# First expert slots five steps sooner, their tables on VectorE, and one test at the kernel's end

## The chip, the cores and the metric

The kernel runs on one core of a Trainium2 chip. The metric is the device time of one execution in microseconds (us). The kernel before takes 1280.56 us (median of three runs, 1279.65 to 1280.75).

## The reference, cut to what matters

Attention of 8 batches x 8 heads over 576 tokens with head size 64, in which each query keeps its 32 best keys, and then a mixture of 8 experts with one expert per token:

```python
scores = scale * (q @ k.T)                       # 576 x 576 for each batch and head
mask = scores >= (32nd largest of the row)
attn = softmax(where(mask, scores, -1e9)); o = attn @ v
x = o, heads side by side                        # 4608 tokens x 512
logits = x @ w_gate; e = argmax(logits); p = softmax(logits)[e]
out[tok] = p * sigmoid(x[tok] @ w_output_gate[:, e]) * (relu(x[tok] @ w1[e]) @ w2[e])   # 512 -> 1024 -> 512
```

## The kernel before, in words

**The loop.** The 4608 tokens are 36 query tiles of 128, and a step takes one pair of heads of one tile, so there are 144 steps (`NSTEP`), and the loop over `i` (L873) runs four more for what trails. Everything is written into the engines' instruction streams in the order of this loop; each engine runs its own stream in order and waits for the others by semaphores. In a step VectorE finds each row's 32nd largest score: `rank` (six MAX8 at L308 and four MATCH_REPLACE at L311, here for step i; the first L308 of six marks a step's start), `window` (two MAX8 at L350, step i-1), `gmax` (sixteen MAX8 at L301, step i+1), `choose` (two small operations at L361, step i-1; in calm steps also L365, a limit for ScalarE) and `weigh` (L377, which drops the scores below the limit and sums the rest). ScalarE copies the scores from PSUM (L282), makes marks (L335), takes the exponentials (L345, in calm steps L393 for the second head) and copies the turned probabilities (L412). GpSimd (POOL in the profile) adds the marks to the scores (L338, two additions a step). TensorE makes the scores (L274), turns the probabilities (`flip`, L404) and in every second step multiplies them with v (`attend`, L436).

**Calm steps.** In the steps below `LONE` (= 4 x 7 + 20 = 48) the second head's mask is not made by VectorE's `weigh` but by ScalarE (L384) and GpSimd (L387, the addition of `veil`), which saves VectorE one L377 a step. TensorE has no expert work in these steps.

**Routing.** When a tile's four steps are done, its gate logits are made (L466, L475 on TensorE, `tile_rows` on VectorE). `SORTS` names after which tiles the tokens so far are sorted by expert: the groups end at tiles 7, 10, 12 and so on, with 3, 2, 3 ... slots each, and after the last tile come `USUAL` = 11 slots (40 in all). A slot is 128 tokens of one expert. For a group, `group_route` is some 22 small VectorE operations (L520 to L566), and `slot_table` (L581) some 28 dependent operations on a few numbers that say which expert a slot has and where its tokens lie. The table runs on GpSimd for the nine groups inside the loop, and on VectorE for the last. `queue_slots` then appends the slots to `order`.

**What sets the order.** Small operations stand in queues: `fill(n)` writes n of them from `urgent`, then `small`, into VectorE's stream at the place where it is called: in a calm step four after `choose` and four at the step's end (L951, L960). `later("ids", ...)` (L863) puts work on GpSimd under a budget per step (`run_slow`). `side` holds TensorE work of the router.

**A slot's work.** Once in `order`, a slot passes through `ahead(...)`: list of tokens (`id`), weights (`w1`, `w2`, 2 MB each by SyncE's queue), the rows (`x`, a gather of GpSimd), the turned rows (`turn`, L703 on TensorE). `ahead("x", fetch_x, 2, "id", 2)` says that x is fetched two steps after id at the soonest. Then `heavy_start` puts four pieces in a queue and the loop takes one per step (`heavy_piece`): two up products (L714, 32 matmul records each) and two down products (L729, eight records). The output is scattered by GpSimd (L740).

**The tail.** After the loop come the heavy pieces left, then the other slots in `slots_in_turn`, with weights and rows split in two parts of lower precision (ScalarE L1008, VectorE L1009, products L1036). At the very end `unsettled` counts rows whose 32nd largest is not certain. Then every engine loads `need` (L1155) and branches if more than the usual 11 last slots are called for (L1157), and loads `flag` (L1171) and branches if a row was unsettled (L1173), in which case all is done again exactly. With the data of this benchmark neither branch's body runs.

Of the kernel before, what the change touches and what calls it, by code (L numbers as in the profile page):

```python
# [13 lines left out]
I32 = mybir.dt.int32  # L14
# [12 lines left out]
SORTS = ((7, 3, 112), (10, 2, 96), (12, 3, 120), (15, 3, 80), (17, 4, 96), (20, 1, 128), (23, 4, 112), (27, 4, 128),  # L27
# [12 lines left out]
def tile_topk_attention_moe(  # L40
# [65 lines left out]
    before = consts.tile([P, P], F32, name="before")  # L106
# [23 lines left out]
    def setup():  # L130
# [5 lines left out]
        def gates():  # L136
            for a in range(2):
# [8 lines left out]
        ops = [lambda: nc.gpsimd.memset(wg, 0.0), gates,  # L146
               lambda: nc.gpsimd.memset(ones, 1.0), lambda: nc.gpsimd.memset(ones_b, 1.0),
               iota(before, [[1, P]], 0, -1),
               lambda: nc.gpsimd.tensor_scalar(before_b, before, 0.0, None, op0=ALU.is_gt),
# [12 lines left out]
    flag = consts.tile([1, 1], I32, name="flag")  # L162

    def unsettled(cp, pp):
# [17 lines left out]
        nc.vector.tensor_copy(flag, total)  # L182

    def run(exact, stack):
# [11 lines left out]
        pools = {"p": ps_m}  # L196
# [118 lines left out]

        def lone(i, a):
            return a == 1 and not exact and i < LONE
# [263 lines left out]
        def slot_table(g, last):  # L581
# [3 lines left out]
            eng = nc.vector if last else nc.gpsimd  # L585
# [30 lines left out]
            if last:  # L616
                def count():
                    NEED.append(st.tile([1, 1], I32, name="need"))
                    eng.tensor_copy(NEED[0], T["d"][:, 7 + E:8 + E])
                add(count)  # L620
# [7 lines left out]
            for k in (4, 2, 1):  # L628
                for nm in ("past", "way"):
                    add(lambda nm=nm, k=k: eng.tensor_tensor(T[nm][:, :n, 0:k], T[nm][:, :n, 0:k], T[nm][:, :n, k:2 * k],  # L630
                                                             op=ALU.add))
            add(lambda: eng.tensor_scalar(tl("slot", [1, 2, MAXS])[:, 0, :n], T["past"][:, :n, 0], float(E - 1), None,
                                          op0=ALU.min))
            add(lambda: eng.tensor_tensor(T["way"][:, :n, 0], T["way"][:, :n, 0], slot_off[:, :n], op=ALU.add))
            add(lambda: eng.tensor_tensor(T["slot"][:, 1, :n], T["way"][:, :n, 0],
                                          first_row[:, 0:1].to_broadcast([1, n]), op=ALU.add))
            def slots():
                SLOT[g] = st.tile([1, 2, MAXS], I32, name="slots", bufs=3)
                eng.tensor_copy(SLOT[g][:, :, :n], T["slot"][:, :, :n])
# [19 lines left out]
        gbuf = [mp.tile([P, DM], F32, name=f"xg{g}", bufs=1) for g in range(NGB)]  # L659
        for x in gbuf:  # L660
            nc.gpsimd.memset(x, 0.0)
# [4 lines left out]
        def fetch_w1(s, g, k, rows):  # L666
            ev = nc.values_load(SLOT[g][0:1, 0, k:k + 1], engines=[SP], min_val=0, max_val=E - 1,
                                skip_runtime_bounds_check_because="clamped to the last expert")
            a = mp.tile([P, NC, FF], F32, name="w1t", bufs=2)
# [3 lines left out]
        def fetch_w2(s, g, k, rows):  # L673
            ev = nc.values_load(SLOT[g][0:1, 0, k:k + 1], engines=[SP], min_val=0, max_val=E - 1,
                                skip_runtime_bounds_check_because="clamped to the last expert")
            b = mp.tile([P, NF, DM], F32, name="w2t", bufs=2)
# [3 lines left out]
        def fetch_id(s, g, k, rows):  # L680
# [3 lines left out]
            it = mp.tile([P, 4], I32, name="idt", bufs=NLIST)  # L684
# [14 lines left out]
        def turn(s, pool, name):  # L699
# [4 lines left out]
            def ev():  # L704
                XS[s] = mp.tile([P, NC, P], F32, name="xs", bufs=2)
                nc.scalar.activation(XS[s], px, AF.Copy)
# [11 lines left out]
        def up(s, f0):  # L718
            if f0 == 0:
                HT[s] = mp.tile([P, NF, P], F32, name="ht")  # L720
# [11 lines left out]
        def put(s):  # L732
            it = G[s][0]
            flush("out")
            y = mp.tile([P, DM], F32, name="y", bufs=2)
# [16 lines left out]

        LONE = 4 * ENDS[0] + 20 if ENDS else 0
# [119 lines left out]
        for i in range(NSTEP + 4):  # L873
# [6 lines left out]
            calm = i < LONE and not exact  # L880
# [26 lines left out]
            elif 2 <= i < LONE:  # L907
# [25 lines left out]
            if ev:  # L933
                late.append(ev)
# [283 lines left out]
```

## Time and profile before

| | |
|---|---|
| median of three runs | 1280.56 us (1279.65 to 1280.75) |
| the profiled execution | 1277.66 us, span 1275.8 us |
| busy share of the span | TensorE (PE) 92%, VectorE (DVE) 94%, ScalarE (ACT) 82%, GpSimd (POOL) 59% |
| TensorE's granted clock | 0.986 of full speed in the mean |
| HBM | 178 GB/s over the span |

Busy times of all engines but TensorE are those of instructions, not of useful work: an instruction that is held up while it runs counts as busy. TensorE's matmuls are pipelined and their ends modelled, so its waits tell more than its busy time. The span is 1.9 us shorter than the execution's own time.

### The profile page before, as it was taken

What the parts mean: (1) busy time and instruction counts of PE and PEld (TensorE: products, weight loads), DVE (VectorE), ACT (ScalarE), POOL (GpSimd) and SP (SyncE); (2) the same over time, 40 slices, a digit from 0 to 9 for tenths busy, and PEclk for the clock granted to TensorE, in tenths of its full rate; (3) what the DMA queues carried; (4) which work ended last, traced back from release to release, by engine and by line L of the source; (5) the groups of instructions that cost most, each with busy time, mean ns of one, the idle gap of its engine ahead of it and who ended that gap; (6) DMA issues with size and microseconds to landing.
All of it is one profiled execution on the core that took longest, in us unless ns stands there. A gap on an engine that the chain in (4) does not pass through costs nothing. (4 is left out here: it accounts for less than half of the span.)

```text
span 1275.8 us, 31308 instructions
## 1 busy us (share of the span) xinstructions
PE 1179.8 (92%) x9792; PEld 898.1 (70%) x9792; DVE 1197.4 (94%) x6154; ACT 1043.8 (82%) x1984; POOL 755.4 (59%) x1221
## 2 busy tenths in 40 slices
PE   6888778677799999999999999999999999999995
PEld 5665656555577777777777777777777777788884
DVE  7999999999999999999999999999999974898884
ACT  6999999898888878788888888888888863888883
POOL 6666666698775766756767667567657743311210
PEclk8999999999799999999999999999999999999998
DMA  5400210202818562765565565765554467999980
GB/s 138 77 18 25 65 55 18 55 19 64 289 54 279 199 228 106 242 228 158 173 204 158 210 208 156 263 221 185 192 176 150 157 233 251 380 396 378 382 312 32
DMA packets 109383, 227.47 MB, mean 178 GB/s; under 512 B 14858, under 2 KB 33546, under 8 KB 108176
## 3 DMA queue, kind: packets, MB, share of 16 engines
q1 hardware_dynamic: 99536, 205.67, 48.1%
q0 software_dynamic: 7552, 18.96, 4.4%
q8 instruction: 81, 1.33, 0.5%
q10 hardware_dynamic: 2112, 0.68, 0.3%
q14 instruction: 102, 0.84, 0.2%
HBM read 206.68 MB, written 20.69 MB: 178 GB/s over the span
## 5 line engine op out<-in xcount | busy, mean ns | idle before, releaser
L338 POOL TENSOR_TENSOR w<-s,marks 128x576 f32<-128x576 f32 x288 | 362.9, 1281 | 181.7 <-ACT marks L335 171.2
L301 DVE MAX8 cand<-s 128x8 f32<-128x72 f32 x2304 | 322.1, 218 | 9.7 <-ACT s L282 9.7
L404 PE MATMUL pst<-ident,ep 128*128 128x128 f32 x1296 | 207.0, 284 | 55.1 <-ACT ep L393 47.1
L335 ACT ACTIVATE marks<-s,v 128x576 int8<-128x576 f32 x288 | 220.9, 770 | 35.8 <-DVE v L308 31.9
L404 PEld LDWEIGHTS pst<-ident,ep 128*128 128x128 f32 x1296 | 145.9, 142 | 142.5 <-ACT ep L393 57.8
L412 ACT ACTIVATE pT<-pst 128x512 f32<-128x512 f32 (+1 forms) x432 | 197.8, 481 | 7.0 <-PE pst L404 4.6
L350 DVE MAX8 v<-w 128x8 f32<-128x576 f32 x288 | 202.2, 744 | 0.0
L282 ACT ACTIVATE s<-ps 128x1152 f32<-128x1152 f32 (+1 forms) x145 | 162.3, 1120 | 45.5 <-PE ps L274 44.2
L714 PE MATMUL pm<-xs,w1t 128*128 128x128 f32 x1664 | 194.7, 275 | 0.9 <-issue 0.8
L714 PEld LDWEIGHTS pm<-xs,w1t 128*128 128x128 f32 x1664 | 189.9, 192 | 1.4 <-issue 1.1
L377 DVE SCALAR_TENSOR_TENSOR ep<-s,kth,ep 128x576 f32<-128x576 f32 x240 | 188.0, 812 | 0.3 <-issue 0.3
L274 PE MATMUL ps<-kst,qst 64*128 64x288 f32 (+1 forms) x1280 | 181.4, 432 | 5.4 <-ACT s L282 5.4
L436 PE MATMUL po<-pT,v 128*64 128x128 f32 (+3 forms) x3200 | 185.1, 266 | 0.0
L436 PEld LDWEIGHTS po<-pT,v 128*64 128x64 f32 (+1 forms) x3200 | 157.8, 136 | 33.0 <-issue 31.3
L729 PE MATMUL pm<-w2t,ht 128*128 128x512 f32 x400 | 180.4, 594 | 0.0
L345 ACT ACTIVATE ep<-s,v 128x576 f32<-128x576 f32 x240 | 175.4, 778 | 0.0
L740 POOL DMA_INDIRECT out_dram<-y,idt x40 | 45.4, 1136 | 184.6 <-ACT y L736 167.3
L308 DVE MAX8 v<-cand 128x8 f32<-128x64 f32 x864 | 148.3, 213 | 0.0
L274 PEld LDWEIGHTS ps<-kst,qst 64*128 64x128 f32 (+1 forms) x1280 | 98.2, 178 | 44.6 <-issue 16.2
L729 PEld LDWEIGHTS pm<-w2t,ht 128*128 128x128 f32 x400 | 72.2, 190 | 72.4 <-issue 72.4
L311 DVE MATCH_REPLACE8 cand<-v,cand 128x64 f32<-128x64 f32 x576 | 116.2, 209 | 0.0
L387 POOL TENSOR_TENSOR w<-s,marks 128x576 f32<-128x576 f32 x48 | 61.5, 1280 | 52.7 <-ACT marks L384 52.4
(182 smaller groups left out, 1838.0 us busy)
## 6 DMA issues: line engine op xcount, KB each, us to landing
w1t<-in_w_dram SPq DMA_DIRECT2D x40, 2048.0 KB
w2t<-in_w_dram SPq DMA_DIRECT2D x40, 2048.0 KB
v<-in_va_dram SPq DMA_DIRECT2D x8, 1152.0 KB
x_rows<-xu SPq DMA_DIRECT2D x36, 256.0 KB
qst<-in_qa_dram SPq DMA_DIRECT2D x70, 128.0 KB
kst<-in_ka_dram SPq DMA_DIRECT2D x14, 576.0 KB
ids<-far SPq DMA_DIRECT2D x1, 678.0 KB
xg<-x_rows,idt POOLq DMA_INDIRECT x40, 6.7
```

Of the source, the lines that this page charges most:

```text
L274: nc.tensor.matmul(ps[qs, a, n, :288], Q[t][rows, hp, qs], K[b][rows, hp, cols], start=True, stop=True)
L301: nc.vector.max(out=c[:, 8 * g:8 * g + 8], in_=SC[i, a][:, g * GW:(g + 1) * GW])
L335: nc.scalar.activation(m.bitcast(I8).rearrange("p (s b) -> p s b", b=2)[:, :, 1], s, AF.Sign, bias=vs[:, a, PIVOT - 1:PIVOT], scale=-(1.0 ...
L338: nc.gpsimd.tensor_tensor(w, s, m, op=ALU.add)
L345: nc.scalar.activation(EP[i][:, a, :], SC[i, a], AF.Exp, bias=VV[i][0][:, a, 32:33], scale=SCALE)
L350: nc.vector.max(out=VV[i][0][:, a, 24:32], in_=SW[i][0][a])
L377: nc.vector.scalar_tensor_tensor(e, SC.pop((i, a)), kth_col(i, a), e, op0=ALU.is_ge, op1=ALU.mult, accum_out=SM[t][:, 2 * hp + a:2 * hp + ...
L404: nc.tensor.transpose(ps[:, c - c0, :], pt[:, c * P:(c + 1) * P], ident)
L412: nc.scalar.activation(x, ps[:, :n, :], AF.Copy)
L436: nc.tensor.matmul(po[a * 64:(a + 1) * 64, k, qs], lhs, rhs, start=half and not k and not m, stop=(c == 3 and k == 1 and m == len(TT[t]) - 1))
L714: nc.tensor.matmul(ph[:, f - f0, :], w[:, c, f * P:(f + 1) * P], XS[s][:, c, :], start=(c == 0), stop=(c == NC - 1))
L729: nc.tensor.matmul(PY[s], HT[s][:, f, :], w[:, f, :], start=(f == 0), stop=(f == NF - 1))
```

## The change

- `SORTS`: the second group ends at tile 9 rather than 10.
- The tables of the first two groups (those that are made while `order` is empty) go into `small`, so VectorE runs them, in 28 operations (one reduction takes the place of three halvings). Later groups stay on GpSimd.
- A calm step writes up to eight small operations between `choose` and `weigh`, none at its end. `calm` now means that no slot has begun (`cur[0]` is 0), so it ends where the first slot begins.
- Until the first slot has begun, `x` and `turn` follow one step behind what they need rather than two.
- After the loop the next slot's rows are turned while the last heavy piece is still to come; the first slot in `slots_in_turn` asks for `w1` only two ahead, and splits the next slot's `w1` after both of its up halves (`late`).
- `over` counts the extra slots called for, `flag[0]` is unsettled rows plus `over`, `flag[1]` the unsettled rows. At the end there is one test, of `flag[0]`; the test for extra slots and that for the exact pass stand inside its body.

The core of the difference:

```diff
-SORTS = ((7, 3, 112), (10, 2, 96), (12, 3, 120), (15, 3, 80), ...
+SORTS = ((7, 3, 112), (9, 2, 96), (12, 3, 120), (15, 3, 80), ...
...
-        nc.vector.tensor_copy(flag, total)
+        nc.vector.tensor_copy(flag[:, 1:2], total)
+        nc.vector.tensor_tensor(total, total, over, op=ALU.add)
+        nc.vector.tensor_copy(flag[:, 0:1], total)
...
         def lone(i, a):
-            return a == 1 and not exact and i < LONE
+            return a == 1 and i in CALM
...
-        def slot_table(g, last):
+        def slot_table(g, last, soon=False):
...
-            eng = nc.vector if last else nc.gpsimd
+            eng = nc.vector if last or soon else nc.gpsimd
...
+                    if not exact:
+                        eng.tensor_scalar(over, T["d"][:, 7 + E:8 + E], -float(usual), 0.0, op0=ALU.add, op1=ALU.max)
...
-                ahead("turn", lambda s, *_: evs.append(turn(s, ps_t, "pst")), 1, "x", 2)
+                pool, name = (ps_t, "pst") if heavy else (ps_m, "pm")
+                ahead("turn", lambda s, *_: evs.append(turn(s, pool, name)), 1, "x", 2 if heavy else 1)
...
-                ops = slot_table(g, False)
+                ops = slot_table(g, False, not order)
+                if not order:
+                    small.extend(ops)
+                    ops = []
...
-            calm = i < LONE and not exact
+            calm = not exact and i < NSTEP and not cur[0]
+            if calm:
+                CALM.add(i)
...
-                fill(4 if calm else 1)
+                fill(8 if calm else 1)
                 weigh(i - 1)
-            ahead("x", fetch_x, 2, "id", 2)
+            ahead("x", fetch_x, 2, "id", 2 if heavy else 1)
...
-            fill(4 if calm else 3)
+            if not calm:
+                fill(3)
...
-                    ahead("w1", fetch_w1, 3)
+                    ahead("w1", fetch_w1, 2 if late else 3)
...
-                    splitted(s + 1, 0, 0)
+                    if not late:
+                        splitted(s + 1, 0, 0)
                     up_half(s, 1)
                     yield
                     turned(2)
-                    splitted(s + 1, 0, 1)
+                    for half in range(2):
+                        splitted(s + 1, 0, half)
+                    late = False
...
         while heavy:
             background()
             fetch_ahead()
+            if len(heavy) == 1:
+                ahead("turn", lambda s, *_: turn(s, ps_t, "pst")(), min(1, had["x"] - cur[0]))
...
-        if usual < NLAST:
+        def more():
             need = nc.values_load(NEED[0], ...)
             with tc.If(need > usual):
...
-        run(False, stack)
-    many = nc.values_load(flag[0:1, 0:1], min_val=0, max_val=2 * P, ...)
+        more = run(False, stack)
+    many = nc.values_load(flag[0:1, 0:1], min_val=0, max_val=2 * P + NLAST, ...)
     with tc.If(many > 0):
-        with ExitStack() as stack:
-            run(True, stack)
+        more()
+        bad = nc.values_load(flag[0:1, 1:2], ...)
+        with tc.If(bad > 0):
+            with ExitStack() as stack:
+                more = run(True, stack)
+            more()
```

What this does to the order of the steps, read from the two programs: before, the first slots are queued in step 45 and the first slot's pieces start in step 51, then every fourth step (55, 59, ... 147), 25 slots in the loop of which the last has three pieces left after it. Now they are queued in step 43 and start in step 46, then 50, 54, 58, 62, 67, 71 and so on to 107, then 112, 116 to 144: 25 slots, all within the loop; steps 66 and 111 have no piece. Steps 0 to 46 are calm (before 0 to 47). The router of the second group starts in step 41 (before 44).

VectorE in calm step 37, here before the change: after the last `choose` operation (L361) and the limit for ScalarE (L365), `weigh` (L377) comes at once, and then the next step's `rank`.

```order
L301 MAX cand<-s 128x8 x16
L361 SCALAR_TENSOR_TENSOR x_4332,kth<-left,n,v_4093 128x8
L361 SCALAR_TENSOR_TENSOR x_4334,kth<-left,n,v_4093 128x8
L365 TENSOR_SCALAR less<-kth 128x1
L377 SCALAR_TENSOR_TENSOR ep,sums<-s,kth,ep 128x576
L308 MAX v_4313<-cand 128x8 x2
```

The same place with the change (`choose` is now L367, the limit L371, `weigh` L383):

```order
L367 SCALAR_TENSOR_TENSOR x_4343,kth<-left,n,v_4094 128x8
L367 SCALAR_TENSOR_TENSOR x_4345,kth<-left,n,v_4094 128x8
L371 TENSOR_SCALAR less<-kth 128x1
L615 TENSOR_TENSOR sl_past<-slot_iota,pad_d 1x24
L618 TENSOR_SCALAR sl_past<-sl_past 1x24
L620 TENSOR_SCALAR first_row<-pad_d 1x8
L621 TENSOR_TENSOR first_row<-first_row,done_121 1x8
L629 TENSOR_TENSOR sl_jump<-first_row 1x8
L630 TENSOR_SCALAR sl_jump<-sl_jump 1x8
L633 TENSOR_TENSOR sl_way<-sl_past,sl_jump 1x24
L640 TENSOR_REDUCE sl_slot<-sl_past 1x3
L383 SCALAR_TENSOR_TENSOR ep,sums<-s,kth,ep 128x576
```

Eight operations of the first group's table now stand between the limit and `weigh`; in other steps from 33 to 46 it is none to eight, of the router and the tables.

TensorE at the end of the loop, before: the first two rows are half a down product and the last rows of the router, then come the last slot's up product and its down products after the loop.

```order
L729 MATMUL pm<-w2t,ht 128x512 x4
L466 MATMUL pst<-xT,wg 32x128 x4
L457 MATMUL pst<-ident,xT 128x128 x2
L714 MATMUL pm<-xs,w1t 128x128 x16
L475 MATMUL pst<-ident,lt 128x128
L457 MATMUL pst<-ident,xT 128x128 x2
L714 MATMUL pm<-xs,w1t 128x128 x16
```

And with the change (L753 is the down product, L738 the up product, L1045 the turn of a slot's rows for the tail):

```order
L753 MATMUL pm<-w2t,ht 128x512 x4
L472 MATMUL pst<-xT,wg 32x128 x4
L463 MATMUL pst<-ident,xT 128x128 x2
L753 MATMUL pm<-w2t,ht 128x512 x4
L481 MATMUL pst<-ident,lt 128x128
L463 MATMUL pst<-ident,xT 128x128 x2
L738 MATMUL pm<-xs,w1t 128x128 x16
L1045 MATMUL pm<-ident,xg_125 128x128 x4
```

Where the 25th slot's up products stood stand now its down products, and the 26th slot's first up product.

## Rows read from the trace of the kernel before

**Rows 1.** Stages: stretch, busy us of PE, PEld, DVE, ACT, POOL; PEclk, DMA share, GB/s.

```profile
351.00:1030.00 679.00, 679.00 (x5970) 508.09 (x5970) 677.40 (x3863) 558.43 (x1138) 451.98 (x776) 1.00 0.57 187
```

**Rows 2.** TensorE's waits up to 345 us: what for, us, times, longest.

```profile
PE pst L404 <- ACT ep L393: 47.1, 36, 2.6
```

**Rows 3.** TensorE's timeline: start us, duration, operation; steps 51, 143, loop's end.

```profile
351.67 3.74 PE L714 MATMUL pm<-xs,w1t 128*128 128x128 f32 x32
355.24 0.60 PE L404 MATMUL pst<-ident,ep 128*128 128x128 f32 x4
...
1034.63 3.74 PE L714 MATMUL pm<-xs,w1t 128*128 128x128 f32 x32
...
1047.22 3.60 PE L729 MATMUL pm<-w2t,ht 128*128 128x512 f32 x8
...
1051.10 0.60 PE L703 MATMUL pst<-ident,xg 128*128 128x128 f32 x4
```

**Rows 4.** The page's costliest groups: busy us, mean ns, idle before; `attend` on TensorE.

```profile
L436 PE MATMUL po<-pT,v 128*64 128x128 f32 (+3 forms) x3200 | 185.1, 266 | 0.0
```

**Rows 5.** VectorE's timeline: first L308 of steps 28, 32, 35, 41, 43, 46, 51.

```profile
188.36 0.35 DVE L308 MAX8 v<-cand 128x8 f32<-128x64 f32 x2
...
214.25 0.35 DVE L308 MAX8 v<-cand 128x8 f32<-128x64 f32 x2
...
238.59 0.34 DVE L308 MAX8 v<-cand 128x8 f32<-128x64 f32 x2
...
277.96 0.34 DVE L308 MAX8 v<-cand 128x8 f32<-128x64 f32 x2
...
292.10 0.34 DVE L308 MAX8 v<-cand 128x8 f32<-128x64 f32 x2
...
312.29 0.34 DVE L308 MAX8 v<-cand 128x8 f32<-128x64 f32 x2
...
350.14 0.34 DVE L308 MAX8 v<-cand 128x8 f32<-128x64 f32 x2
```

**Rows 6.** VectorE's timeline, tail: first and seventeenth operation of the last table.

```profile
1067.33 0.15 DVE L598 TENSOR_TENSOR sl_cnt<-base,carry 1x8 f32<-1x8 f32 x1
...
1070.56 0.24 DVE L630 TENSOR_TENSOR sl_past<-sl_past 1x92 f32<-1x92 f32 x1
```

**Rows 7.** Timeline, calm step 38: VectorE's limit for ScalarE, GpSimd's `veil`.

```profile
263.78 0.15 DVE L365 TENSOR_SCALAR less<-kth 128x1 f32<-128x1 f32 x1
...
264.96 1.27 POOL L387 TENSOR_TENSOR w<-s,marks 128x576 f32<-128x576 f32 x1 [0.17 <-issue]
```

**Rows 8.** Timeline, step 33: a small operation of VectorE beside GpSimd's `veil`.

```profile
229.43 1.25 DVE L559 TENSOR_SCALAR den<-den 128x7 f32<-128x7 f32 x1
...
229.37 1.28 POOL L387 TENSOR_TENSOR w<-s,marks 128x576 f32<-128x576 f32 x1 [1.93 <-ACT marks L384]
```

**Rows 9.** VectorE's groups of operations, 351 to 1030: busy us, mean ns.

```profile
L377 DVE SCALAR_TENSOR_TENSOR ep<-s,kth,ep 128x576 f32<-128x576 f32 x182 | 141.8, 815 | 0.3 <-issue 0.3
...
L361 DVE SCALAR_TENSOR_TENSOR x<-left,n,v 128x8 f32<-128x8 f32 x182 | 54.1, 333 | 0.0
```

**Rows 10.** TensorE's waits, 1072 to 1100 us: what for, us, times, longest.

```profile
PE pst L1052 <- ACT hs L1045: 2.4, 1, 2.4
...
PE pm L714 <- issue: 0.8, 1, 0.8
```

**Rows 11.** Timeline, GpSimd: the last scatter.

```profile
1264.89 0.98 POOL L740 DMA_INDIRECT out_dram<-y,idt  x1 [6.64 <-ACT y L736]
```

**Rows 12.** Lines of the two tests: ns shortest/median/longest, first and last start us.

```profile
L1157 POOLq EVENT_SEMAPHORE  x5: 17/43/3069, 1265.7 to 1269.1; - x5
L1157 PEldq COMPARE_BRANCH  x1: 3924/3924/3924, 1264.4 to 1264.4; - x1
...
L1171 POOLq TENSOR_LOAD <-flag x1: 305/305/305, 1269.6 to 1269.6; - x1
...
L1173 POOLq EVENT_SEMAPHORE  x6: 17/30/43, 1273.1 to 1273.6; - x6
```

More of the change, by code (lines that the diff above doesn't have):

```diff
@@ L160, in setup @@
         return ops
-    flag = consts.tile([1, 1], I32, name="flag")
+    flag = consts.tile([1, 2], I32, name="flag")
+    over = consts.tile([1, 1], F32, name="over")
+    nc.gpsimd.memset(over, 0.0)
     def unsettled(cp, pp):
@@ L658, in run, with row_buffers @@
         NGB = 3
-        gbuf = [mp.tile([P, DM], F32, name=f"xg{g}", bufs=1) for g in range(NGB)]
-        for x in gbuf:
-            nc.gpsimd.memset(x, 0.0)
+        gbuf = []
+        def row_buffers():
+            gbuf[:] = [pools["mp"].tile([P, DM], F32, name=f"xg{g}", bufs=1) for g in range(NGB)]
+            for x in gbuf:
+                nc.gpsimd.memset(x, 0.0)
+        row_buffers()
         W, G, XS, HT, PY = {}, {}, {}, {}, {}
@@ L906, in run @@
                 early.append(attend(i - 4))
-            elif 2 <= i < LONE:
+            elif calm and 2 <= i:
                 idle = ps_m.tile([P, 4, P], F32, name="pm")
@@ L931, in run @@
                 (last if calm else late).append(flip(i - 2, 2))
-            ev = turn_ahead() if room else None
+            ev = turn_ahead() if room or not heavy else None
             if ev:
-                late.append(ev)
+                (last if calm else late).append(ev)
             for f in early:
@@ L1139, in run @@
             background()
+        settled = exact
+        if not settled and small_end is None and not small:
+            unsettled(st, ps_o)
+            settled = True
         for _ in slots_in_turn():
@@ L1157, in run, with one @@
             with tc.If(need > usual):
-                for k in range(usual, NLAST):
-                    def one():
-                        order.append((NGRP - 1, k, N))
-                        for _ in slots_in_turn():
-                            pass
-                    if k == usual:
-                        one()
-                    else:
-                        with tc.If(need > k):
+                with ExitStack() as own:
+                    pools["mp"] = own.enter_context(tc.tile_pool(name="mp3", bufs=1))
+                    pools["w"] = own.enter_context(tc.tile_pool(name="mp4", bufs=2))
+                    pools["t"] = own.enter_context(tc.tile_pool(name="ps_t3", bufs=2, space=PSUM))
+                    pools["m"] = own.enter_context(tc.tile_pool(name="ps_m3", bufs=1, space=PSUM))
+                    pools["p"] = own.enter_context(tc.tile_pool(name="ps_e3", bufs=4, space=PSUM))
+                    row_buffers()
+                    for k in range(usual, NLAST):
+                        def one():
+                            order.append((NGRP - 1, k, N))
+                            for _ in slots_in_turn():
+                                pass
+                        if k == usual:
                             one()
+                        else:
+                            with tc.If(need > k):
+                                one()
+        return more if usual < NLAST else lambda: None
     with ExitStack() as stack:
-        run(False, stack)
-    many = nc.values_load(flag[0:1, 0:1], min_val=0, max_val=2 * P,
-                          skip_runtime_bounds_check_because="a count of partitions, twice")
+        more = run(False, stack)
+    many = nc.values_load(flag[0:1, 0:1], min_val=0, max_val=2 * P + NLAST,
+                          skip_runtime_bounds_check_because="a count of partitions, twice, and of slots")
     with tc.If(many > 0):
-        with ExitStack() as stack:
-            run(True, stack)
+        more()
+        bad = nc.values_load(flag[0:1, 1:2], min_val=0, max_val=2 * P,
+                             skip_runtime_bounds_check_because="a count of partitions, twice")
+        with tc.If(bad > 0):
+            with ExitStack() as stack:
+                more = run(True, stack)
+            more()
 def kernel(**inputs):
```

66 lines of the change are left out of this document (39 added, 27 removed).

## The prediction

> **What bounds the kernel now.** I read the table by stages first, then the waits of TensorE, then the timelines of the places that the change touches. From 351 to 1030 us TensorE is busy for 679.00 of 679 us at a granted clock of 1.00 [rows 1], and the view of waits has no wait of TensorE in that stretch: from the first expert slot on, TensorE sets the pace. VectorE looks as full there (677.40), but part of that is hold-up inside instructions: the small L361 has a mean of 333 ns [rows 9] where operations as small take about 200 [rows 6, 7], some 24 us over its 182 instructions. Before 345 us it is the other way round: TensorE waits for ScalarE's exponentials (47.1 us in 36 waits, [rows 2]), which wait for VectorE's thresholds, so VectorE's steps set the pace there. The change moves the border between these two stretches from step 51 to step 46, so its worth is VectorE's time that is saved ahead of the border, less TensorE's work that comes behind it. After the loop TensorE is the bound again with little waiting, and the end is a chain on GpSimd.
>
> **Prices of one step.** In step 51 the first up product takes 351.67 to 355.24 = 3.57 us; the one of step 143 starts at 1034.63 [rows 3], 92 steps and 682.96 us later, so a step takes 7.42 us. A down product's modelled duration is 3.60 against 3.74 for an up product, so 3.43, and the mean piece is 3.50. Turning a slot's rows is 0.60 in every fourth step, 0.15 a step. Attention's share of TensorE is therefore 7.42 - 3.50 - 0.15 = 3.77 us a step. A calm step of VectorE is (214.25 - 188.36)/4 = 6.47 us [rows 5].
>
> **1. The first slot's start on VectorE's side.** Step 46 started at 312.29 and step 51 at 350.14 [rows 5]. How much later does step 46 start now?
> - *The first group's table on VectorE, 28 operations.* The last table shows the like: sixteen from 1067.33 to 1070.56 [rows 6], 0.20 each, so 28 x 0.20 = 5.6.
> - *Hold-ups.* `veil`'s addition on GpSimd (L387) starts 1.18 us after the limit (263.78 to 264.96, [rows 7]). Today `weigh` runs in that time and the next operations rarely meet it. With up to eight small operations in between they do. The nearest row is L559: 1.25 us long, and it ends with the L387 that started just before it [rows 8]; its like beside nothing takes 0.2, so a hold-up costs 1.05 to 1.1. Five calm steps carry most of the table; I take 3.5 hold-ups, 3.9 us.
> - *GpSimd relieved.* Today the table runs on GpSimd in steps 41 and 42, which take 292.10 - 277.96 = 14.14 [rows 5], where two calm steps are 12.9: 1.2 us go.
> - *The second group's router,* 13 operations before step 46. Today the first group's router, 22 operations in steps 32 to 34, makes these 238.59 - 214.25 = 24.34 where three calm steps are 19.4, so 5.0 us or 0.23 each, hold-ups included. 13 of them are 3.0; some 1.0 of router work in steps 44 and 45 today and of one hold-up fewer in the first router comes off: 2.0.
>
> Together 5.6 + 3.9 - 1.2 + 2.0 = 10.3 later: step 46 starts at 322.6, which is 27.5 us before step 51 did. Bounds: 41 operations at their own duration of 0.15 and no hold-up, less 1.2 and some 0.6 of second-router work that stands there today, give 4.4; 0.20 each with a hold-up in seven steps, less 1.2, gives 14.3.
>
> In [rows 8] GpSimd was first, by 0.06 us, and VectorE waited to its end.
>
> The Trainium skill's page "SBUF — State Buffer", section "SBUF: two separate sides", says that VectorE operations with two SBUF inputs and GpSimd share a port pair as an exclusive lock, which the first holds for its whole instruction. By that rule each of the five table steps meets the lock, 1.6 us more than I take, and the sum would end near 1274.3.
>
> **2. Attention's work behind the border.** TensorE now has the attention of steps 46 to 50 inside its full stretch: 5 x 3.77 = 18.9. `attend` falls on even steps, and three of these five are even; one is 185.1/72 = 2.57 us [rows 4], so half of one more: +1.3. The pieces of the 25 slots are 100 in both kernels (three of them after the loop today, none now), so they cost the same. Sum +20.2.
>
> **3. Idle TensorE in steps 46 to 50.** These steps are not calm any more, so each has a second `weigh` (0.815, [rows 9]): 5 x 7.27 = 36.3 for VectorE, and some 33 operations of the second router and table are spread over them; not each waits for the one before, so 0.16 each, 5.3: 41.6. TensorE has 20.2 + 5 x 3.50 + 0.8 for turns = 38.5. It waits for the difference, +3.0 (bounds 0, where its queue already trails, and 8, at 0.23 each with hold-ups and the first rows late).
>
> **4. Two steps without a piece,** 66 and 111. There TensorE has 3.50 us less to do. It runs dry only as far as it does not trail VectorE; it trails in a step by no more than 7.42 - 7.27 = 0.15 before hold-ups, hence some 3 us over twenty steps if no hold-up eats it. I take half covered: +3.5 (bounds 0 and 7.0).
>
> Ahead of the tail the change is thus -27.5 + 20.2 + 3.0 + 3.5 = -0.8.
>
> **5. Start of the tail.** TensorE waits there for 2.4 us for ScalarE's hidden rows and 0.8 for an unturned slot [rows 10]; ScalarE's queue had a `w1` split ahead of them that waited for its transfer. The next slot's rows are turned sooner now and that split comes later: -3.2 (bounds 0 and -4). The last table's one operation more (0.15) falls into a stretch where TensorE has products to do.
>
> **6. One test fewer.** The last scatter starts at 1264.89 [rows 11]; GpSimd then waits up to 3.07 us in the test for extra slots, loads `flag` at 1269.6, and starts on the other side of its second branch at 1273.1 [rows 12]. TensorE's branch alone takes 3.9 us in the first test. With one test there is one such jump; the scatter's landing runs beside it. I take the step from the first wait's start, 1265.7, to the second load, 1269.6: -3.9. Bounds -0.7, where landing and jump come one after the other, and -4.4. The two operations on `flag` (0.3 us) end before GpSimd, at its last scatter, gets to the load, so they cost nothing; without that cover 0.3.
>
> **The sum.** -0.8 - 3.2 - 3.9 = -7.9. The profiled execution took 1277.66 (span 1275.8 and 1.9 around it), so its like would take 1269.8; the median of the runs is 2.9 above that execution, and with the same difference 1280.56 becomes **1272.7**. What a measurement can tell from no change is about 0.2%, 2.6 us: faster means under 1278.0, slower over 1283.1.
>
> **Rivals.**
> - *More is given.* The table's operations cost no more than their own 0.15 and meet no hold-up (term 1 at 4.4, 5.9 less), and TensorE trails enough to cover the steps without a piece (3.5 less): 1263.3. For it: TensorE has no wait at all behind the border today. Against: the row of 1.25 us. 15%.
> - *The test that goes had only the landing in it.* If GpSimd must first see the scatter land, then jump, the end saves 0.7: 1272.7 + 3.2 = 1275.9. For it: its 3.07 us wait begins at 1265.7 and the jump of its second branch takes 3.2 (1269.9 to 1273.1) with nothing to wait for. Against: TensorE's 3.9 us branch ends at 1268.3, at the same time as that wait. 17%.
> - *VectorE has no slack behind the border:* terms 3 and 4 at their upper bounds, 5.0 + 3.5 more: 1281.2, no change. For it: 677.40 busy of 679. Against: 24 us of that is hold-up that comes only where it fits. 10%.
> - *The first slot doesn't start in step 46.* Tokens, rows and turn follow one step apart now, while 8 MB of weights start in the same step; if the rows are late by a step, the border is step 47: +6.5, 1279.2. 5%.
> - *Slower: VectorE and GpSimd hold each other up wherever small operations move.* The table and router at 14.3 (+4.0), steps 46 to 50 at 8 (+5.0), and hold-ups eat what TensorE trails, so that both empty steps are idle (+3.5): 12.5 more, 1285.2. It decides from 10.5 us of extra loss. For it: steps 32 to 34, where 22 operations cost 5.0 us. Against: outside calm steps there is no `veil`, and most operations stand beside nothing. 9%.
>
> The forecast itself keeps 44%, by itself from 1268.5 to 1276.5. Faster: 44 + 15 + 17 = 76%. Within 0.2%: 10 + 5 = 15%. Slower: 9%. A range from 1263.5 to 1281.2 leaves out the last and about half of the first and third rival, and the tails of the forecast.
>
> **What would show it.** Step 46's first rank near 322.6 and its up product within 2 us of it; no wait of TensorE from there on but some 3 us up to step 50 and some 2 each in steps 66 and 111; small operations beside L387 with 1.1 to 1.3 us in three or four of steps 34 to 40; the loop's last `weigh` near 1041; from the last scatter's end to the end of the span 6 us rather than 10. Wrong would be: the first piece after 330, or waits of TensorE of over 10 us between 322 and 1030, or an end as long as today's.

## The result, and the profile after

| | before | after |
|---|---|---|
| median | 1280.11 us (4 runs, 1279.18 to 1280.75) | 1297.3 us (4 runs, 1293.62 to 1299.43) |
| ratio | | 1.0136, 95% interval 1.0113 to 1.0160 |
| profiled execution, span | 1277.66, 1275.8 | 1297.55, 1295.7 |

The change makes the kernel slower by 1.4%; 1272.7 was forecast. I follow the 19.9 us between the two spans from place to place.

**Ahead of the first piece** the forecast was too dark. VectorE's timeline of the kernel after shows the first rank of steps 46 to 49, 51 and 143 (L312 is now what L308 was):

```profile
313.49 0.34 DVE L312 MAX8 v<-cand 128x8 f32<-128x64 f32 x2
...
320.22 0.35 DVE L312 MAX8 v<-cand 128x8 f32<-128x64 f32 x2
...
331.72 0.34 DVE L312 MAX8 v<-cand 128x8 f32<-128x64 f32 x2
...
344.66 0.33 DVE L312 MAX8 v<-cand 128x8 f32<-128x64 f32 x2
...
361.41 0.33 DVE L312 MAX8 v<-cand 128x8 f32<-128x64 f32 x2
...
1048.68 0.35 DVE L312 MAX8 v<-cand 128x8 f32<-128x64 f32 x2
```

Step 143 in the kernel before:

```profile
1032.65 0.35 DVE L308 MAX8 v<-cand 128x8 f32<-128x64 f32 x2
```

Step 46 starts 1.2 us later than before [rows 5], where 10.3 were expected. Step 51 is then 11.3 later, and step 143 is 16.0 later. The hold-up of VectorE that was priced at 1.1 us and expected in three or four calm steps happens once up to step 46. VectorE's and GpSimd's timelines in step 37:

```profile
255.35 1.24 DVE L612 TENSOR_TENSOR pad_b<-pad_a 1x8 f32<-1x8 f32 x1
```
```profile
255.31 1.27 POOL L393 TENSOR_TENSOR w<-s,marks 128x576 f32<-128x576 f32 x1 [0.15 <-ACT marks L390]
```

The two meet more often than that, but then it is GpSimd that waits. In step 38 `veil` starts just before VectorE's `weigh` (L383), and is 0.8 us longer than alone:

```profile
264.25 2.06 POOL L393 TENSOR_TENSOR w<-s,marks 128x576 f32<-128x576 f32 x1 [0.16 <-ACT marks L390]
```
```profile
264.36 0.80 DVE L383 SCALAR_TENSOR_TENSOR ep<-s,kth,ep 128x576 f32<-128x576 f32 x1
```

The same happens in steps 35, 39, 40 and 43 (1.62 to 1.82 us); in the kernel before no `veil` is longer than 1.30. VectorE has no wait from 225 to 313 us, so these five cost it no wait there.

**Steps 46 to 49** are where the first large piece goes: they last 6.73, 11.50, 12.94 and 8.68 us. The timelines of TensorE, ScalarE and VectorE in these steps, with each wait in brackets:

```profile
319.56 3.84 PE L738 MATMUL pm<-xs,w1t 128*128 128x128 f32 x32
...
326.26 0.66 PE L410 MATMUL pst<-ident,ep 128*128 128x128 f32 x4 [1.98 <-ACT pT L418]
329.00 0.47 PE L410 MATMUL pst<-ident,ep 128*128 128x128 f32 x1 [2.09 <-ACT ep L399]
...
330.48 5.36 PE L738 MATMUL pm<-xs,w1t 128*128 128x128 f32 x32
```
```profile
323.44 0.60 ACT L746 ACTIVATE ht<-pm 128x512 f32<-128x512 f32 x1 [4.25 <-PE pm L738]
323.93 0.77 ACT L390 ACTIVATE marks<-s,less 128x576 int8<-128x576 f32 x1
324.60 1.12 ACT L286 ACTIVATE s<-ps 128x1152 f32<-128x1152 f32 x1
...
335.88 0.60 ACT L746 ACTIVATE ht<-pm 128x512 f32<-128x512 f32 x1 [3.11 <-PE pm L738]
```
```profile
325.75 2.25 DVE L305 MAX8 cand<-s 128x8 f32<-128x72 f32 x16 [2.35 <-ACT s L286]
...
328.75 1.30 DVE L367 SCALAR_TENSOR_TENSOR x<-left,n,v 128x8 f32<-128x8 f32 x1
...
338.68 2.25 DVE L305 MAX8 cand<-s 128x8 f32<-128x72 f32 x16 [3.79 <-ACT s L286]
340.85 1.18 DVE L618 TENSOR_SCALAR sl_past<-sl_past 1x16 f32<-1x16 f32 x1
```

The three engines wait for each other in a ring. ScalarE's queue has the up product's result (L746) ahead of the next copy of scores (L286), so it stands 4.25 us until TensorE is through with the product; VectorE then waits 2.35 for the scores, and TensorE 2.09 for exponentials. In the second round it is 3.11 and 3.79. Beside the ring, six small operations of VectorE in steps 46 to 50 are held up, such as L367 and L618 above, which end as a GpSimd addition (L344) ends; together they are some 4.6 us longer than their like. The clock is lower too, as the stages of these steps show (columns as in [rows 1]):

```profile
324.00:330.00 6.00, 1.93 (x17) 0.84 (x15) 4.25 (x20) 5.44 (x12) 3.93 (x5) 0.75 0.25 74
330.00:336.00 6.00, 6.00 (x41) 6.00 (x38) 4.79 (x30) 2.17 (x6) 1.27 (x4) 0.68 0.01 0
```

The granted clock is 0.75 of the upper level in the stage with the waits and 0.68 in the next, and the second up product takes 5.36 us instead of 3.74 [rows 3].

**The two steps without a piece** leave TensorE idle, and are together no shorter for VectorE. The stages are steps 66, 111 and 112:

```profile
473.70:481.70 8.00, 5.34 (x60) 4.13 (x56) 7.97 (x45) 6.82 (x14) 5.25 (x8) 1.00 0.79 249
...
808.40:815.50 7.10, 3.71 (x31) 2.17 (x29) 7.10 (x43) 6.12 (x14) 5.12 (x7) 0.98 1.01 376
815.50:824.90 9.40, 9.40 (x87) 7.88 (x87) 8.71 (x46) 5.99 (x12) 4.83 (x6) 0.84 1.04 272
```

TensorE is busy for 5.34 of 8.00 and 3.71 of 7.10 us, VectorE throughout. Steps 66 and 111 take 15.2 us together; with a piece, in the kernel before, they took 15.0. After the second the clock is 0.84 and the step lasts 9.40.

**The start of the tail** is the largest piece. Timelines of SyncE, ScalarE, TensorE and VectorE there:

```profile
1082.43 0.34 SPq L488 DMA_DIRECT2D x_rows<-xu  x1
...
1083.34 0.39 SPq L694 DMA_DIRECT2D w1t<-in_w_dram  x1
```
```profile
1091.84 1.91 ACT L1038 ACTIVATE w1h<-w1t 128x2048 fp32r<-128x2048 f32 x1 [8.20 <-DMA w1t<-in_w_dram]
```
```profile
1078.91 0.27 PE L481 MATMUL pst<-ident,lt 128*128 128x128 f32 x1
...
1094.78 0.79 PE L1066 MATMUL pm<-w1h,xsh 128*128 128x512 f32 x1 [7.57 <-ACT xsh L1038]
...
1098.35 0.63 PE L1066 MATMUL pm<-w1l,xsh 128*128 128x512 f32 x1
1098.78 0.63 PE L1066 MATMUL pm<-w1h,xsl 128*128 128x512 f32 x1
...
1128.28 0.66 PE L1082 MATMUL pst<-ident,hs 128*128 128x128 f32 x4 [3.32 <-ACT hs L1075]
```
```profile
1058.51 0.08 DVE L383 DVE_READ_ACCUMULATOR ep<-s,kth,ep 128x1 f32 x1
...
1080.10 0.29 DVE L498 TENSOR_TENSOR tl<-pst,r 128x128 f32<-128x128 f32 x1 [19.14 <-ACT xu L466]
...
1105.10 0.18 DVE L659 CAST slots<-sl_slot 1x46 int32<-1x46 f32 x1
```

VectorE ends the loop's last `weigh` at 1058.5. TensorE then still has the rest of the last steps and the 25th slot's four pieces, and gets to the last tile's rows (L481) at 1078.9. SyncE's queue stores these rows before it asks for the next slot's weights (1082.43, 1083.34); ScalarE waits 8.20 us for them. TensorE has only the 26th slot's two up products to bridge that and stands for 7.57 us; then the products run 0.43 us apart up to 1101.8 and 0.23 apart from there on (the granted clock is 0.53 in the mean from 1094.78 to 1102.29). The last table's operations stand in VectorE's stream behind the splits of the late weights, so the last slots are known at 1105.1 (before, the like came right after [rows 6], some 33 us sooner), and TensorE waits again, 2.1 and 3.3 us.

It is not the way to the last rows that has become longer. In the kernel before, four pieces stand ahead of them too (steps 144 to 147), and VectorE waits for them as long, 19.43 against 19.14 us. What differs is what TensorE has behind them: before, it is the 25th slot's three pieces that are left, the two down products among them, and then the 26th slot's. VectorE and TensorE before:

```profile
1063.43 0.29 DVE L492 TENSOR_TENSOR tl<-pst,r 128x128 f32<-128x128 f32 x1 [19.43 <-ACT xu L460]
```
```profile
1066.32 7.11 PE L729 MATMUL pm<-w2t,ht 128*128 128x512 f32 x16
```

The chain of waits of the kernel after goes through the late weights, as three of its pieces show:

```profile
1083.34 8.25 DMA w1t<-in_w_dram
...
1105.20 4.49 DVE w2l L1039 x2
1110.57 15.18 DMA w1t<-in_w_dram
```

**The end** is as forecast: GpSimd's timeline and the test's lines,

```profile
1288.51 0.98 POOL L764 DMA_INDIRECT out_dram<-y,idt  x1 [6.64 <-DVE flag L186]
```
```profile
L1222 POOLq TENSOR_LOAD <-flag x1: 515/515/515, 1288.4 to 1288.4; - x1
...
L1224 POOLq EVENT_SEMAPHORE  x6: 17/30/777, 1292.2 to 1293.4; - x6
```

7.2 us from the last scatter's start to the end of the span, where it was 10.9 [rows 11].

### The profile page after: what moved, and what is told of

It is laid out like the page before. It is cut to its first block, busy times and chain, and to the rows that moved or that the text cites. A ratio compares the mean times of both kernels' runs of the same rounds, so it can differ in the third digit from the quotient of the medians.

```text
span 1295.7 us, 31235 instructions
## 1 busy us (share of the span) xinstructions
PE 1186.3 (92%) x9768; PEld 900.0 (69%) x9768; DVE 1207.8 (93%) x6210; ACT 1042.8 (80%) x1982; POOL 744.0 (57%) x1157
## 4 chain that ended last, share of the span: by engine, by line
DVE 76%; PE 17%; DMA 2%; issue 2%; ACT 2%; POOL 0%; SPq 0%; POOLq 0%; ACTq 0%
DVE cand L305 23%; DVE v L356 14%; DVE ep L383 12%; PE pm L1066 11%; DVE cand L315 8%; DVE v L312 8%; DVE x L367 5%; DMA w1t<-in_w_dram 2%; PE pm L738 2%; DVE lg L500 1%; PE pst L1082 1%; DMA xg<-x_rows,idt 1%; PE po L442 1%; DVE tl L498 1%; PE pm L753 1%
## 5 line engine op out<-in xcount | busy, mean ns | idle before, releaser
L344 POOL TENSOR_TENSOR w<-s,marks 128x576 f32<-128x576 f32 x288 | 362.9, 1281 | 194.5 <-ACT marks L341 190.4
L286 ACT ACTIVATE s<-ps 128x1152 f32<-128x1152 f32 (+1 forms) x145 | 162.4, 1120 | 43.6 <-PE ps L278 43.3
L738 PE MATMUL pm<-xs,w1t 128*128 128x128 f32 x1664 | 196.4, 277 | 0.0
L738 PEld LDWEIGHTS pm<-xs,w1t 128*128 128x128 f32 x1664 | 191.7, 193 | 0.4 <-issue 0.4
L383 DVE SCALAR_TENSOR_TENSOR ep<-s,kth,ep 128x576 f32<-128x576 f32 x241 | 188.7, 812 | 0.0
L753 PE MATMUL pm<-w2t,ht 128*128 128x512 f32 x400 | 180.3, 593 | 0.0
L312 DVE MAX8 v<-cand 128x8 f32<-128x64 f32 x864 | 148.1, 213 | 0.0
L753 PEld LDWEIGHTS pm<-w2t,ht 128*128 128x128 f32 x400 | 72.1, 190 | 71.9 <-issue 71.9
```

The lines of the kernel that those rows point to most:

```text
L312: nc.vector.max(out=vs[:, a, 8 * r:8 * r + 8], in_=cs[a])
L344: nc.gpsimd.tensor_tensor(w, s, m, op=ALU.add)
L383: nc.vector.scalar_tensor_tensor(e, SC.pop((i, a)), kth_col(i, a), e, op0=ALU.is_ge, op1=ALU.mult, accum_out=SM[t][:, 2 * hp + a:2 * hp + ...
L738: nc.tensor.matmul(ph[:, f - f0, :], w[:, c, f * P:(f + 1) * P], XS[s][:, c, :], start=(c == 0), stop=(c == NC - 1))
L753: nc.tensor.matmul(PY[s], HT[s][:, f, :], w[:, f, :], start=(f == 0), stop=(f == NF - 1))
```

## The experiments

Theory A: the loss comes from where the pieces stand, in three places (steps 46 to 49, the steps without a piece, the tail's start behind the last rows). Theory B, the rival on the slower side: small operations on VectorE and GpSimd hold each other up. Theory C: the new rule for the tail's first slot is what delays it. Ratios are to the kernel before, run on the same chips.

**No pieces in steps 144 to 147.**

```diff
-            ev = heavy_piece()
+            ev = heavy_piece() if i < NSTEP else None
```

> Edit: the changed kernel, but no expert piece is taken in the four steps after the last (steps 144 to 147); the last slot's four pieces run after the loop. Theory A (backlog: the last tile's rows stand behind four pieces on TensorE, the next weights are asked for behind the store of these rows on SyncE's queue, so the tail starts late): the store of the last rows, at 1082.4 now, comes some 14 us sooner, TensorE's wait of 7.6 us at 1087 goes, and the time falls by 10 to 18 us from 1297.3, to about 1283. Theory B (VectorE and GpSimd hold each other up wherever small operations were moved): the tail is not the place, the time stays within 3 us of 1297. Theory C (the new rule for the weights and splits of the tail's first slot delays it): within 3 us of 1297, and the wait stays.

Measured: 1280.79 us, ratio 1.0032 (1.0020 to 1.0044), so 1.04% or 13 us less than after. TensorE's last rows and SyncE's next `w1`:

```profile
1068.47 0.33 PE L481 MATMUL pst<-ident,lt 128*128 128x128 f32 x1 [0.43 <-ACT lt L476]
```
```profile
1062.73 8.34 SPq L488 DMA_DIRECT2D x_rows<-xu  x2
1076.43 0.39 SPq L694 DMA_DIRECT2D w1t<-in_w_dram  x1
```

The rows come 10.4 us sooner and the wait of 7.6 us is gone; from 1060 to 1130 TensorE's longest wait is 1.8. The step order of the loop is untouched (step 143 starts at 1050.2, 1.5 later than after), so the 13 us are the tail's alone. Theory A holds here; by B and C the time would have stayed. The edit brings the rows forward and at once puts four pieces behind them, so by itself it doesn't tell these two apart; the run with the order of before, further down, and the equal waits of VectorE above speak for the pieces behind.

**The first piece back in step 51.**

```diff
-            calm = not exact and i < NSTEP and not cur[0]
+            calm = not exact and i < 48
...
-            if heavy or when.get(("turn", s), clock[0]) >= clock[0]:
+            if heavy or when.get(("turn", s), clock[0]) >= clock[0] or step[0] < 51:
```

> Edit: the changed kernel, with calm steps 0 to 47 and the first piece not before step 51, as in the kernel before; tables, groups, lags, tail and tests stay changed. Theory A (the loss comes from where the pieces stand: in steps 46 to 49, in two steps without a piece, and at the tail's start): with the pieces back in place the time is that of before less the 3.7 us of the single test, 1274 to 1279. Theory B (small operations on VectorE): they stay, so 1290 or more. Theory C (rule of the tail's first slot): stays, so 1285 to 1292.

Measured: 1279.59 us, ratio 1.0022 (1.0012 to 1.0031). Most of the loss is gone, against B and C; but it was to be 3.7 us faster than before and is 2.8 slower, so A left out 6.5 us. In the profiled executions 5.3 of these stand at step 143 already (1037.9 against 1032.7): 1.4 at step 46, 2.8 at step 51, the rest over the 92 steps that follow.

**The first piece in step 48, after two steps without one.** The same two lines with `i < 46` and `step[0] < 48`.

> Edit: the changed kernel, with calm steps 0 to 45 and the first piece not before step 48, so two steps without pieces stand between the calm steps and the first piece; by the program all steps from 48 to 147 then have a piece. Theory A: steps 46 to 49 lose 3 rather than 10 us, the two steps without a piece (7 us of TensorE, 2 to 3 more after them) are gone, the tail still starts late: 1297 - 6 - 9 = 1282, bounds 1278 to 1287. Theory B: within 3 us of 1297. Theory C: within 3 us of 1297.

Measured: 1288.3 us, ratio 1.0089 (1.0072 to 1.0106), 0.47% less than after (9.0 us between the two profiled spans). The loop's end profits (step 143 at 1039.4, 9.3 sooner than after), and the tail stays as it is: TensorE waits 7.5 us for the first split weights there, as after.

**The tail's first slot as before.**

```diff
-            late = True
+            late = False
```

> Edit: the changed kernel, with the tail's first slot as before (weights asked three ahead, the next slot's w1 split between its up halves). Theory A: the weights come late whatever the rule, so within 3 us of 1297. Theory B: the same. Theory C: 1285 to 1290.

Measured: 1292.29 us, ratio 1.0122 (1.0103 to 1.0140). The interval overlaps that of after, so the rule's worth is not told from nothing; theory C falls. (In the single profiled executions the stretch from step 143 to the end is 3.9 us shorter than after; with both edits, further down, the same line makes it 1.2 longer.)

**Both edits.** First piece in step 48, last four pieces after the loop.

> Edit: the changed kernel with both edits of the runs before: first piece in step 48 with calm steps 0 to 45, and no piece in steps 144 to 147 (the last slot's four run after the loop). Theory A (three separate places): the two gains add, 0.0047 and 0.0104 of the time, so the ratio to before is about 0.9985 (1274.6, bounds 1270 to 1278). If the tail's idle time was only the other side of the first loss, and one edit does for both: 1.003, 1280. Theory B (small operations on VectorE cost 10 us or more): not below 1.003.

Measured: 1272.52 us, ratio **0.9964** (0.9950 to 0.9978): faster than both kernels, 1.7% below after. The two gains add; the 0.0021 beyond their sum lies within the intervals. TensorE's stages from 1060 on:

```profile
1060.00:1080.00 20.00, 20.00 (x140) 15.85 (x139) 11.16 (x51) 6.20 (x9) 9.02 (x16) 1.00 0.67 187
1080.00:1100.00 20.00, 18.27 (x88) 14.64 (x87) 16.59 (x13) 15.66 (x15) 1.83 (x1) 1.00 0.97 360
1100.00:1120.00 20.00, 18.90 (x96) 15.60 (x95) 18.00 (x13) 17.26 (x18) 8.57 (x6) 1.00 1.04 404
```

The clock is 1.00 throughout, and 2.8 us of TensorE are idle, where the kernel after has 14 us idle from 1080 to 1140.

**The same with the tail's first slot as before.** Both of the edits above and `late = False`.

> Edit: the first run of this set (first piece in step 48, last four pieces after the loop) with the tail's first slot as before (weights three ahead, split between the up halves). The rule is worth -1.8 +- 3 us in the changed kernel; with TensorE busy at that place theory A expects no difference from the first run by more than 2 us; theory C (the new rule delays the weights) 3 to 5 us less.

Measured: 1272.82 us, 0.9964 (0.9951 to 0.9976), no difference.

**The single test alone.** The edits that put all else back are those of the expectation.

> Edit: the changed kernel with everything but the single test at the end put back (second group at tile 10, tables on GpSimd, four and four small operations, calm steps 0 to 47, first piece in step 51, lags of two steps, the tail's first slot as before). Theory A: the test alone gives 3.7 us, as the last scatter's start to the end was 7.2 rather than 10.9 us in the profile: ratio 0.9971. If the landing of the last scatter or the work beside it takes the test's place: 0.999 to 1.001.

Measured: 1276.61 us, 0.9989 (0.9977 to 1.0001): not told from no change, and less than the 3.7 us. From the last scatter's start (1268.7) to the end (1274.5) it is 5.8 us, 5.1 less than before, but the scatter comes 3.8 later; 1.6 of that stand at step 143, where single executions of the same loop differ by up to 1.5. The rest shows in this run's own trace. The run is not the single test alone: it keeps a part of the change that the list of the change leaves out, the count of unsettled rows (L172 to L186), which stands ahead of the tail here, in the run with the first piece in step 51 and in all with the last pieces after the loop. The kernel before has it at its very end, and so has the kernel after. Here TensorE waits for it, and the up product behind it is slow (granted clock 0.69 from 1077.67 to 1083.1):

```profile
1076.20 0.19 PE L181 MATMUL po<-lo,ones 128*1 128x2 f32 x2 [1.13 <-DVE lo L179]
...
1077.67 5.47 PE L738 MATMUL pm<-xs,w1t 128*128 128x128 f32 x32 [0.69 <-ACT xs L730]
```

The rows' turn ahead of this product starts 3.1 us later than its like in the kernel before, and what follows the product 4.6 us later. So the count and the slow product cost some 3 us, of which 0.8 are won back by the last scatter. A run with the test alone and the count at the end was not made.

**That, and no pieces in steps 144 to 147.** (The 25th slot then moves into the tail's split products.)

> Edit: the run with only the single test, and no piece in steps 144 to 147. Theory A: the last tile's rows come some 12 us sooner on TensorE, but in the kernel before TensorE idles only some 3 us at the tail's start, so at most 3 us more are won: ratio 0.995 to 0.9975. If VectorE's end of the loop bounds the tail here too: 10 us, 0.989.

Measured: 1273.76 us, 0.9976 (0.9964 to 0.9987), 0.0013 less than without, with overlapping intervals. In the order of before the four pieces ahead of the last rows are hardly in the way: there are others behind the rows.

**The two tests again,** in the fastest kernel.

```diff
+    more()
     many = nc.values_load(flag[0:1, 0:1], ...
     with tc.If(many > 0):
-        more()
         bad = ...
```

> Edit: the run with the first piece in step 48 and the last four after the loop (ratio 0.9964), with the test for extra slots moved back out, ahead of the test of the flag. Theory A: the single test is worth what the ends of the profiles show, 3.7 to 5 us: ratio 0.9993 to 1.0003, and from the last scatter's start to the end 11 us rather than 6. If the test alone is worth only the 1.4 us that the run with nothing else showed: 0.9975.

Measured: 1277.13 us, 0.9996 (0.9984 to 1.0008), 0.0032 or 4.1 us more than with one test. The last scatter's start to the end of the span is 11.2 us (1262.5 to 1273.7) against 6.0 (1264.0 to 1270.0). So the test is worth what the profile said, and it is all that this kernel is seen to win: with two tests, the sooner pieces, well placed, give nothing that can be told.

**How many steps between the calm ones and the first piece,** which stays in step 48. Three runs beside the one with two steps (calm 0 to 45).

> Edit: the same, with calm steps 0 to 46, one step ahead of the first piece. A1: no loss, 0.995 to 0.998. A2: a loss of 2 to 3 us. A3: as the others.

> Edit: the same run (first piece in step 48, last four after the loop) with calm steps 0 to 47 instead of 0 to 45: the first piece stands in the first step that is not calm. Theory A1 (a piece inside a calm step is what costs, because ScalarE's queue there has the up product's result ahead of the copies of scores that VectorE waits for): no loss, ratio 0.995 to 0.998, steps 46 to 50 at 7.5 us or less. Theory A2 (two steps are needed between the calm steps and the first piece, for TensorE to take up what trails): a loss of 4 to 6 us, ratio 0.999 to 1.002. Theory A3 (the small operations of the second group's table in these steps): no difference between this run and the two beside it.

> Edit: the same, with calm steps 0 to 48: the first piece stands in the last calm step, as in the changed kernel, but two steps later. A1 and A2: a loss of 6 to 10 us, ratio 1.001 to 1.005, steps 49 and 50 at 11 to 13 us each. A3: no loss, 0.9964.

| calm steps | first piece | steps 46 to 52 | VectorE waits there | its `choose` and small operations there | ratio |
|---|---|---|---|---|---|
| 0 to 45 | after two steps | 53.9 us | none | 8.5 us | 0.9964 (0.9950 to 0.9978) |
| 0 to 46 | after one step | 56.9 us | none | 12.1 us | 0.9984 (0.9972 to 0.9996) |
| 0 to 47 | next step | 60.2 us | 4.1 us | 11.4 us | 1.0018 (1.0005 to 1.0030) |
| 0 to 48 | in the last calm step | 61.2 us | 4.8 us | 12.1 us | 1.0025 (1.0013 to 1.0038) |

The loss grows with each step that is missing, by 2.6, 4.3 and 0.9 us of the medians; of these the middle one alone is clear of the intervals, but the steps' lengths go the same way. A1, which had no loss unless a piece stands inside a calm step, falls: the next step is almost as bad. The numbers of A2 come out. Its reason, that TensorE must take up what trails, is not shown: with one step between, VectorE waits for nothing and these steps are still 3.0 us longer. What grows there is the time of `choose` and the small operations, by 3.5 us (sums over VectorE's timeline; `weigh` takes 0.7 less). They are the same operations in all four runs, so A3's forecast of no difference falls; but how often they are held up is not the same, and in this run it is the whole loss. VectorE and GpSimd with one step between:

```profile
318.10 1.33 DVE L367 SCALAR_TENSOR_TENSOR x<-left,n,v 128x8 f32<-128x8 f32 x1
```
```profile
316.88 2.52 POOL L344 TENSOR_TENSOR w<-s,marks 128x576 f32<-128x576 f32 x2 [1.78 <-ACT marks L341]
```

With no step between, the waits come on top. In the run with the piece in the next step, VectorE's and TensorE's waits from 313 to 374 us are

```profile
DVE cand L305 <- ACT s L286: 4.1, 2, 2.2
```
```profile
PE pst L410 <- ACT ep L399: 8.7, 4, 3.3
```

and with two steps between VectorE has none and TensorE 4.1 us for L399. Why it takes just two steps was not taken further. Calm step 47 also has transposes on TensorE that nothing reads (L939, 1.5 us), which the runs with calm steps up to 45 and 46 don't have; their part was not tried apart.

## Why the prediction was wrong

The sum by its own steps (us of the profiled executions; pieces that stand elsewhere are taken out, so that the rows add up to the 19.9 but for 0.7 of turns and rounding):

| step of the prediction | forecast | measured |
|---|---|---|
| 1. step 46 against the old step 51 | -27.5 | -36.6 |
| 2. attention behind the border | +20.2 | not measured apart; +20.2 kept in the sum |
| 3. TensorE's excess in steps 46 to 50 | +3.0 | +9.4 (47.9 less 38.5) |
| 4. steps 51 to 142 | +3.5 | +11.8 (4.8 longer, with two pieces, 7.0, fewer) |
| 5. start of the tail | -3.2 | +18.1 |
| 6. one test | -3.9 | -3.7 |

Step 143 to the end takes 247.0 us after and 243.1 before; the kernel after has three pieces less to do there (10.5), so it lost 14.4, which is 18.1 less the 3.7 of the test.

- **Step 5 failed most, and by a sentence of step 2:** "the pieces of the 25 slots are 100 in both kernels (three of them after the loop today, none now), so they cost the same". They take the same time of TensorE, but three of them used to stand behind the last rows, where they bridge the way from the last tile to the next weights; now they stand ahead of the rows, and nothing bridges it. The run with the four pieces after the loop showed it, at 13 us. The forecast had looked for -3.2 from a sooner turn of the next slot's rows and a later split of its weights. The rule for the split is worth nothing that can be told (two pairs of runs), the turn was not run apart, and the 2.4 us wait for hidden rows that was to go is 3.3 us now.
- **Step 4:** half of the two steps' 7 us was to be covered by what TensorE trails. All of it was lost, and more: steps 66 and 111 took as long without a piece as with one, and the step behind the second 1.7 us longer, at the clock of 0.84; the 2.9 us that remain of the 4.8 are spread over the stretch and were not traced. The rival "VectorE has no slack behind the border" was right in this, though its 1281.2 left out the tail. In [rows 1] both engines are full; I took VectorE's hold-ups for slack because they come "only where it fits". They were no slack here: the two steps got no shorter when TensorE had less to do.
- **Step 3** was taken as a difference of two busy sums, 41.6 and 38.5. VectorE was in fact busy for 41.5 us of the 47.9 there, but that the sum agrees is luck: 4.6 of it are six operations held up, which the sum had not. What it had no term for are the 6.1 us that VectorE stands in the ring of waits through ScalarE's queue, which no sum of two engines shows, and the slower clock after it (TensorE stands for 5.9 us and is busy for 42.1 rather than 38.5). The four runs with zero to two steps between show the size of all this, some 8 us; by their table up to 4.8 of it are VectorE's waits and about 3 to 3.5 longer small operations.
- **Step 1** was 9.1 too dark. The table itself cost 5.2 us in steps 37 to 40, near its 5.6; but VectorE was held up once and not 3.5 times, and the first router, written between `choose` and `weigh`, takes 3.3 us less by step 35. Hold-ups became fewer, not more: in steps 33 to 45 of the kernel before five small operations are held up, 4.4 us together, two of them in this router (L559 in [rows 8], and L562 with 1.28 us at 237.26); now it is one, 1.1 us. The rival on the slower side named hold-ups as its mechanism. The time was on its side, mostly for other reasons; in steps 46 to 52 hold-ups have the part just named. The Trainium skill's rule of the shared port pair ("SBUF — State Buffer", section "SBUF: two separate sides") agrees with the row at 255.35, where GpSimd started first and VectorE waited, and with the five steps in which GpSimd waited for `weigh`. Of the five meetings in table steps that I had from the rule four came (steps 37 to 40); what I had wrong is who waits: VectorE only in the first.
- **Step 6** was right: 3.7 in the profile, 4.1 between two kernels that differ in it alone.

The prediction named waits of TensorE of over 10 us between 322 and 1030 as a sign of being wrong, and it came: they add up to 13.5 us, where the kernel before has none from 351 on.

What stays open: some 2 to 4 us that the kernels with nearly everything put back lose between step 46 and the tail, why a missing step between the calm ones and the first piece makes the small operations meet GpSimd more often, and the single test with nothing else beside it.

## What to carry to other kernels

Work that is moved ahead costs the same on its engine, but ask what it used to cover where it stood: filler after the last dependent result is worth most while the next stage's transfers are on their way. Where two engines were both full, taking work from one in single steps gave nothing back. And a new kind of work that started two steps after the change of order was some 8 us cheaper here than in the same step, where small operations were held up and the in-order queue of a third engine tied the two together.

## What was not expected of the hardware

- After two waits of some 2 us on TensorE (busy for 1.93 of 6 us) the granted clock was 0.75 and 0.68 in the mean of two stages, so part of each at 1.2 and part at 2.4 GHz, and an up product took 5.36 us instead of 3.74; after the 7.57 us wait the products ran 0.43 us apart for 7 us, then 0.23.
- Of some 70 small VectorE operations between the limit and `weigh` in steps 33 to 46, one was held up by GpSimd's `veil` (1.24 us); in five of these steps `veil` was held up by `weigh` instead (1.62 to 2.06 us rather than 1.27).
- A branch whose body doesn't run costs: one test at the end is 4.1 us of 1277 between two kernels that differ in it alone, and 5.2 us from the last scatter to the end of their profiles.
